# Opening of an attention and feed-forward kernel: k's first loads in requests of 16 tiles, row sums side by side in matmuls of 512, value products behind the gate's

## The chip, the cores and the metric

One core of one Trainium2 chip. The metric is device time in microseconds of one execution, about 810 us here. A profile is one further execution with its trace; its span (first to last instruction) is about 2 us shorter than the device time. "Seen at" is when an engine starts on loaded data, "landed" is when the load's completion packets are done in the trace, some 0.3 to 0.4 us earlier. "TensorE", "VectorE", "ScalarE" and "GpSimd" are PE, DVE, ACT and POOL in the profile's lines.

## The reference

Inputs are float32: q, k, v of 4 x 6016 x 256 and three feed-forward weights. Cut to what matters:

```python
qn = q / (np.linalg.norm(q, axis=1, keepdims=True) + 1e-06)   # norms over the 6016 rows
kn = k / (np.linalg.norm(k, axis=1, keepdims=True) + 1e-06)
s = kn.transpose(0, 2, 1) @ qn / tau                          # 256 x 256 per batch
a = softmax(s)                                                # written out in the original
x = (v @ a).reshape(B * S, D)
g = x @ w_gate
out = (silu(g) * (x @ w_val)) @ w_out
```

## The kernel before: the parts concerned

The softmax matrix is folded into the two feed-forward weights (Wg and Wv), so most of the time goes to three streams of matmuls: g_ps, v_ps and o_new. They can start only when batch 0's k and q have been loaded, their squares summed, k-transposed-q built, the softmax taken and the first weights folded. That is the opening, some 38 us, and only it is changed. Batches 1 to 3 do the same work in the background.

In the opening q and k are loaded as fp8, 47 tiles of 128 rows each. PSUM, below, is the memory in which the matmuls' results stand. VectorE and ScalarE square pairs of tiles in turn. A matmul with a matrix of ones sums the squares over the partitions:

```python
def first_row_sums(b, t, which, sq, t_last):
    if t == 0:
        ss_new = psum_gv.tile([P, C], FP32, tag="gv"[which])
        state[b, "ss", which] = ss_new
    pm = pairs[t][1]
    for s in range(pm):
        nc.tensor.matmul(state[b, "ss", which], ones_bf, sq[:, s, :],
                         start=(t == 0 and s == 0), stop=(t == t_last and s == pm - 1))

def first_row_copy(b):                       # q's sums so far, as one row
    row = work.tile([1, C], FP32, tag="row")
    nc.vector.tensor_copy(row, state[b, "ss", 0][0:1, :])
    state[b, "row"] = row
```

From q's sixth group on, the sums go into columns instead (`cols`): first the row is turned into columns by 1x1 matmuls, then each further square is added by one-column matmuls. So the row must be there before the last q groups can be summed. The order of loads and work:

```python
kgroups = [(s, min(8, NS - s)) for s in range(0, NS, 8)]   # 8,8,8,8,8,7 tiles
# qgroups come out as 8,8,8,8,4,4,4,2,1 tiles
order = [(g, 1, kgroups) for g in range(NG)] + [(g, 0, qgroups) for g in range(NQ)]
# ... all loads issued by GpSimd in this order, then v's first piece and the weights
G_COLS = NQ - 4
# per group of q: squares, gemm1_pair (k-transposed-q), sums; a reciprocal of k's norms after four of them
```

At the end of the softmax, the row sums of the exponentials and the first folded weights (units 0 and 1 are gate, 2 and 3 value):

```python
row_sum(0)
wp_matmul(b, 0, 0, units[0], lo)
wp_matmul(b, 1, 0, units[1], lo)
wp_matmul(b, 2, 0, units[2], lo)
row_sum(1)
finish_rs(b, rs)
for u, jh in ((0, 1), (1, 1), (2, 1), (3, 0), (3, 1)):
    wp_matmul(b, u, jh, units[u], lo)
```

## Time and profile before

| | before |
|---|---|
| device time, first three runs | 809.96 us median (809.69 to 813.19) |
| span in the profile | 807.6 us |
| TensorE busy | 787.9 us, 98% |
| chain that ended last | TensorE 95%, DMA 3% |
| first g_ps in the records | 37.64 us |
| first v_ps in the records | 37.85 us |

### The profile page before, as it was taken

What the parts mean: (1) busy time and instruction counts of PE and PEld (TensorE: products, weight loads), DVE (VectorE), ACT (ScalarE), POOL (GpSimd) and SP (SyncE); (2) the same over time, 40 slices, a digit from 0 to 9 for tenths busy, and PEclk for the clock granted to TensorE, in tenths of its full rate; (3) what the DMA queues carried; (4) which work ended last, traced back from release to release, by engine and by line L of the source; (5) the groups of instructions that cost most, each with busy time, mean ns of one, the idle gap of its engine ahead of it and who ended that gap; (6) DMA issues with size and microseconds to landing.
All of it is one profiled execution on the core that took longest, in us unless ns stands there. A gap on an engine that the chain in (4) does not pass through costs nothing.

```text
span 807.6 us, 11833 instructions
## 1 busy us (share of the span) xinstructions
PE 787.9 (98%) x3867; PEld 384.4 (48%) x3940; DVE 554.7 (69%) x854; ACT 454.3 (56%) x802; POOL 251.0 (31%) x302
## 2 busy tenths in 40 slices
PE   4999999999999999999999999999999999999998
PEld 3644444444454444444454444444445444444446
DVE  4777878758667878766766778766866665665654
ACT  4666666555556666555555656555555555555553
POOL 4415887332104786332000777610000000000000
PEclk8999999999999999999999999999999999999999
DMA  9995999799886685887976697667556665565443
GB/s 89 143 154 97 147 190 174 144 142 178 149 145 144 131 153 121 152 137 166 145 170 144 113 160 149 131 126 166 128 116 123 144 134 131 125 149 130 117 113 99
DMA packets 203567, 112.43 MB, mean 139 GB/s; under 512 B 151424, under 2 KB 190337, under 8 KB 202753
## 3 DMA queue, kind: packets, MB, share of 16 engines
q1 hardware_dynamic: 185456, 84.55, 44.1%
q0 software_dynamic: 17904, 27.01, 30.6%
q8 instruction: 31, 0.51, 0.3%
q14 instruction: 32, 0.25, 0.1%
q10 hardware_dynamic: 144, 0.10, 0.0%
HBM read 79.06 MB, written 60.48 MB: 173 GB/s over the span
## 4 chain that ended last, share of the span: by engine, by line
PE 95%; DMA 3%; issue 1%; ACT 0%; DVE 0%; POOL 0%; ACTq 0%; POOLq 0%
PE g_ps L458 30%; PE v_ps L458 30%; PE o_new L499 29%; PE ps L425 2%; DMA q_sb<-in_q_dram 2%; PE kq_new L171 2%; PE o_new L552 1%; DMA k_sb<-in_k_dram 1%; ACT silu L464 0%; DVE sv L468 0%; PE ss_new L198 0%; PE last_ps L576 0%; PE unit_ps L425 0%; PE kq_new L176 0%; PE ps L415 0%
## 5 line engine op out<-in xcount | busy, mean ns | idle before, releaser
L468 DVE TENSOR_TENSOR sv<-silu,v_ps 128x512 bf16<-128x512 bf16 (+1 forms) x576 | 386.5, 673 | 214.5 <-ACT silu L464 213.1
L464 ACT ACTIVATE silu<-g_ps 128x512 bf16<-128x512 f32 (+1 forms) x576 | 339.1, 589 | 292.5 <-PE g_ps L458 263.7
L458 PE MATMUL g_ps<-vT,Wg 128*128 128x512 bf16 (+1 forms) x1109 | 326.5, 375 | 1.2
L458 PE MATMUL v_ps<-vT,Wv 128*128 128x512 bf16 (+1 forms) x1104 | 325.1, 374 | 1.0
L499 PE MATMUL o_new<-sv,w_out_sb 128*128 128x512 bf16 (+1 forms) x1079 | 319.1, 375 | 1.4
L458 PEld LDWEIGHTS <-Wv 128*128 128x128 bf16 x1152 | 112.7, 98 | 130.9 <-ACT Wv L437 0.4
L303 POOL TENSOR_TENSOR acc_new<-acc_new,sq 128x512 f32<-128x512 f32 x135 | 157.2, 1165 | 52.6 <-DVE sq L293 37.3
L458 PEld LDWEIGHTS <-Wg 128*128 128x128 bf16 x1152 | 111.3, 98 | 125.8 <-DVE Wv L435 0.2
L499 PEld LDWEIGHTS <-w_out_sb 128*128 128x128 bf16 x1104 | 108.0, 98 | 126.5
L129 POOL DMA_DIRECT2D vb_new<-in_v_dram x47 | 24.2, 516 | 244.9 <-DMA vT<-vb_new 243.8
L509 DVE COPY pl<-o_new 128x512 uint16<-128x512 uint16 (+1 forms) x92 | 62.5, 680 | 14.1 <-ACT pl L508 13.9
L293 DVE TENSOR_TENSOR sq<-q_sb 128x512 bf16<-128x512 fp8e5 x72 | 65.8, 914 | 0.0
L508 ACT COPY pl<-o_new 128x512 uint16<-128x512 uint16 (+1 forms) x92 | 53.1, 578 | 19.8 <-PE o_new L499 19.1
L294 ACT ACTIVATE sq<-k_sb 128x512 bf16<-128x512 fp8e5 x72 | 44.2, 614 | 0.0
L171 PE MATMUL kq_new<-k_sb,q_sb 128*128 128x512 fp8e5 x184 | 28.4, 295 | 1.4 <-DMA q_sb<-in_q_dram 1.3
L114 POOL DMA_DIRECT2D q_sb<-in_q_dram x45 | 25.4, 564 | 11.7 <-DMA k_sb<-in_k_dram 9.8
L198 PE MATMUL ss_new<-sq,ones_bf 128*128 128x256 bf16 x83 | 14.8, 336 | 10.9 <-ACT sq L188 10.9
L171 PEld LDWEIGHTS <-q_sb 128*128 128x256 fp8e5 x184 | 21.2, 137 | 6.3 <-DMA q_sb<-in_q_dram 2.7
L114 POOL DMA_DIRECT2D k_sb<-in_k_dram x42 | 23.2, 554 | 2.9 <-DVE sv L468 1.7
L370 POOL TENSOR_SCALAR den<-th 128x512 f32<-128x512 f32 x3 | 1.8, 614 | 64.4 <-ACT th L369 64.4
L338 POOL TENSOR_TENSOR inv<-inv,half 64x8 f32<-64x8 f32 x3 | 5.0, 1665 | 53.3 <-DVE inv L336 53.3
L298 POOL TENSOR_TENSOR acc_new<-sq 128x512 f32<-128x512 bf16 x3 | 3.5, 1151 | 47.1 <-DVE sq L293 47.1
(90 smaller groups left out, 208.4 us busy)
## 6 DMA issues: line engine op xcount, KB each, us to landing
rows<-pl SPq DMA_DIRECT2D x86, 256.0 KB, 2.6
out_dram<-ot_new SPq DMA_DIRECT2D x43, 512.0 KB, 4.1
vb_new<-in_v_dram POOLq DMA_DIRECT2D x43, 256.0 KB, 4.8
q_sb<-in_q_dram POOLq DMA_DIRECT2D x36, 128.0 KB, 5.9
k_sb<-in_k_dram POOLq DMA_DIRECT2D x33, 128.0 KB, 7.4
ot_new<-rows SPq DMA_TRANSPOSE x92, 3.7
k_sb<-in_k_dram POOLq DMA_DIRECT2D x5, 256.0 KB, 9.0
rows<-pl SPq DMA_DIRECT2D x6, 192.0 KB, 2.4
```

Source lines behind the costliest of these rows:

```text
L114: nc.gpsimd.dma_start(out=dst[:, gs:gs + gm, :], in_=src[b].rearrange("(p s) c -> p s c", s=NS)[:, gs:gs + gm, :])
L129: nc.gpsimd.dma_start(out=vb[:mv, :].rearrange("(p s) c -> p (s c)", s=cm), in_=v[b, cs * P:cs * P + mv, :].rearrange("(p s) c -> p (s c)" ...
L171: nc.tensor.matmul(kq[:, jh, :], q_sb[:, ps:ps + 2, js], k_sb[:, ps:ps + 2, :], start=(t == 0 and jh == 0), stop=last, perf_mode=DR, skip_ ...
L293: nc.vector.tensor_mul(sq[:, :pm, 0, :], q_sb[:, ps:ps + pm, :], q_sb[:, ps:ps + pm, :])
L294: nc.scalar.activation(sq[:, :pm, 1, :], k_sb[:, ps:ps + pm, :], ACT.Square)
L303: nc.gpsimd.tensor_tensor(out=acc, in0=acc, in1=sq[:, s, :, :], op=ALU.add)
L458: nc.tensor.matmul(dst[:, :mv], W[:, kk, fs], vT[:, kk, :mv], start=(kk == 0), stop=(kk == CH - 1))
L464: nc.scalar.activation(silu[:, :mv], g_ps[:, :mv], ACT.Silu)
L468: nc.vector.tensor_mul(sv[:, f, :mv], silu[:, :mv], v_ps[:, :mv])
L499: nc.tensor.matmul(self.o_ps[h][:, :self.mv], w_out_sb[:, f, h * P:(h + 1) * P], self.sv[:, f, :self.mv], start=(f == 0), stop=(f == FH - 1))
L508: nc.scalar.copy(pl[:, 0, :self.mv], halves[:, 0, :self.mv])
L509: nc.vector.tensor_copy(pl[:, 1, :self.mv], halves[:, 1, :self.mv])
```

## The change

Its intent: fewer and larger load requests for k, half as many summing matmuls (each 512 wide, even and odd tiles side by side in one PSUM tile, added at the end), and the gate's folded weights finished before the value's. The large k groups are worked through in fours, so that the four square buffers suffice.

```diff
-            ss_new = psum_gv.tile([P, C], FP32, tag="gv"[which])
+            ss_new = psum_gv.tile([P, 2, C], FP32, tag="gv"[which])
...
-        for s in range(pm):
-            nc.tensor.matmul(state[b, "ss", which], ones_bf, sq[:, s, :],
-                             start=(t == 0 and s == 0), stop=(t == t_last and s == pm - 1))
+        nc.tensor.matmul(state[b, "ss", which][:, :pm, :], ones_bf, sq[:, :pm, :],
+                         start=(t == 0), stop=(t == t_last), skip_group_check=True)
...
-        nc.vector.tensor_copy(row, state[b, "ss", 0][0:1, :])
+        ss = state[b, "ss", 0]
+        nc.vector.tensor_copy(row, ss[0:1, 0, :])
+        nc.vector.tensor_add(row, row, ss[0:1, 1, :])
...
-        first_root(ink, state[b, "ss", 1])
+        ss = state[b, "ss", 1]
+        nc.vector.tensor_copy(ink, ss[:, 0, :])
+        nc.vector.tensor_add(ink, ink, ss[:, 1, :])
+        first_root(ink, ink)
...
-        wp_matmul(b, 2, 0, units[2], lo)
         row_sum(1)
         finish_rs(b, rs)
-        for u, jh in ((0, 1), (1, 1), (2, 1), (3, 0), (3, 1)):
+        for u, jh in ((0, 1), (1, 1), (2, 0), (2, 1), (3, 0), (3, 1)):
...
-    kgroups = [(s, min(8, NS - s)) for s in range(0, NS, 8)]
+    kgroups = [(s, min(16, NS - s)) for s in range(0, NS, 16)]
...
-        if n == 4:
+        if n == 3:
             make_identity(nc, identf)
...   (the loop over groups now takes the pairs of a group in fours: squares, products, sums)
```

More of the change, by code (lines that the diff above doesn't have):

```diff
@@ L680 @@
             first_row_copy(0)
-        sqs = [first_square(0, t, which, on_dve=(t % 2 == 1)) for t in ts]
-        if which == 0:
-            for t in ts:
-                gemm1_pair(0, t)
-            if g == G_COLS:
-                first_cols(0)
-            if g == NQ - 4:
-                keep_warm(1)
-        for t, sq in zip(ts, sqs):
-            if which == 0 and g >= G_COLS:
-                first_col_sums(0, t, sq)
-            else:
-                first_row_sums(0, t, which, sq, (T_COLS if which == 0 else NP) - 1)
+        for at in range(0, len(ts), 4):
+            now = ts[at:at + 4]
+            sqs = [first_square(0, t, which, on_dve=(t % 2 == 1)) for t in now]
+            if which == 0:
+                for t in now:
+                    gemm1_pair(0, t)
+                if g == G_COLS:
+                    first_cols(0)
+                    keep_warm(1)
+            for t, sq in zip(now, sqs):
+                if which == 0 and g >= G_COLS:
+                    first_col_sums(0, t, sq)
+                else:
+                    first_row_sums(0, t, which, sq, (T_COLS if which == 0 else NP) - 1)
         if which == 0:
```

## The prediction

> **What bounds the kernel now.** I read the page first (busy shares, chain by line), then the chain of waits in order of time for the first 70 us, then the timelines of VectorE and GpSimd for the first 40 us.
>
> From the page:
> ```profile
> span 807.6 us, 11833 instructions
> PE 787.9 (98%) x3867; PEld 384.4 (48%) x3940; DVE 554.7 (69%) x854; ACT 454.3 (56%) x802; POOL 251.0 (31%) x302
> PE 95%; DMA 3%; issue 1%; ACT 0%; DVE 0%; POOL 0%; ACTq 0%; POOLq 0%
> ```
> TensorE is the chain for 95% of the span. The change touches none of the matmuls of the three long lines (g_ps, v_ps, o_new); it touches only the opening, in which batch 0's k and q are loaded, squared and multiplied. So the question is by how much the start of the steady stream, the first g_ps, moves.
>
> From the chain of waits in order of time (start us, us, what), the opening:
> ```profile
> 1.93 7.03 DMA k_sb<-in_k_dram
> 9.24 19.08 DMA q_sb<-in_q_dram
> 28.36 1.09 PE kq_new L171 x8
> 29.44 0.89 PE ss_new L198 x8
> 30.33 0.44 PE kq_new L171 x4
> 30.77 0.47 PE ss_new L198 x4
> 31.26 0.42 DVE row L203
> 31.73 0.60 PE cols L211 x4
> 33.06 0.44 PE kq_new L171 x4
> 33.50 0.32 PE cols L221 x8
> ...
> 34.32 0.13 PE cols L221 x6
> ...
> 36.55 0.57 PE unit_ps L425 x5
> 37.12 0.47 PE ps L425 x4
> 37.64 0.38 PE g_ps L458
> ```
> Three stretches. To 28.3 us the loads set the pace. From 28.36 TensorE runs with no gap but one: at 31.26 it waits for VectorE's 0.42 us row copy. From 31.7 to the first g_ps at 37.64 it is continuous. A delay of the row copy therefore reaches the end of the kernel, unless the last q loads are later still.
>
> From VectorE's timeline, the stretch ahead of that copy:
> ```profile
> 22.86 0.29 DVE L233 TENSOR_SCALAR ink<-ink 128x256 f32<-128x256 f32 x1 [0.61 <-ACT ink L228]
> 23.58 1.29 DVE L185 TENSOR_TENSOR sq<-q_sb 128x512 bf16<-128x512 fp8e5 x2 [0.29 <-DMA q_sb<-in_q_dram]
> 28.43 1.29 DVE L185 TENSOR_TENSOR sq<-q_sb 128x512 bf16<-128x512 fp8e5 x2 [0.66 <-DMA q_sb<-in_q_dram]
> 30.65 0.54 DVE L238 RECIPROCAL ink<-ink 128x64 f32<-128x64 f32 x1
> 31.26 0.41 DVE L203 COPY row<-ss_new 1x256 f32<-1x256 f32 x1
> ```
> VectorE spends 1.29 + 0.55 = 1.84 us of each 2.46 us group of q and idles some 0.6; but from 28.43 to the copy it has almost no idle time, and its last reciprocal ends at 31.19, just ahead of the copy.
>
> **What the Trainium skill says.** (1) "DMA: Bandwidth & Descriptors", section "Where 436 GB/s comes from", puts the ceiling of the path into SBUF at 435.2 GB/s. TensorE sees q groups at 23.50, 25.94 and 28.36, so 2.43 us per 8 tiles, or 1.049 MB of float32 read: 432 GB/s. The trace agrees, so bigger requests can't make the stream much faster. (2) The same page's "Anatomy of one DMA" gives about 2 us fixed cost per DMA, mostly the receipt. Here that is hidden by requests queued behind: the last three 8-tile k groups are seen every 2.4 to 2.5 us, with no 2 us holes. (3) "TensorE: Matmul & The Clock Gate", section "Back-to-back issue gap", gives N/2.4 + 2.5 ns: 109 ns for 256 columns, 216 for 512. The chain has 0.89/8 = 111 ns, and 0.43/2 = 215 ns in the steady pairs. It agrees, so one matmul of 512 costs what two of 256 cost. (4) The same page's Part 1 has a clock that halves after sparse activity. The trace has a mean clock of 0.50 from 15 to 20 us, 0.87 from 20 to 25 and 1.00 after, so low only while loads pace the work.
>
> **The change part by part.**
>
> *k in 16s.* 3 loads in place of 6. The bytes are the same. A 7-tile group cost about 0.30 us less than an 8-tile one (its requests' landings 2.16 against 2.46 us apart), so 8 tiles are about 2.40 and a request costs some 0.05 us of its own, which is my estimate. Three fewer: q about 0.15 us earlier, the last k too. Against it: the first squares start one group later (about 9 in place of 6.56 us), and the last k group, now 15 tiles seen at about 18.4, needs 4 squares on each engine: 4 x 0.64 = 2.6 us on VectorE, to 21.0 at best, and 21.3 if its four square buffers wait for a slow TensorE. q's first group is seen at 20.85. So VectorE starts on q's squares at most 0.4 us late.
>
> *Sums side by side.* In the steady q groups 8 matmuls of 256 (0.89 us) become 4 of 512 (4 x 0.216 = 0.86): 0.03 saved. On the chain are one group of 8 and one of 4: about 0.05 us. The weight loads halve, but they are under the matmuls already.
> Two sums are added on VectorE. For k: a copy and an add of 128x256 float32, each about 0.42 (the 128x256 products from PSUM take 0.40 to 0.43). For q: an add of 1x256 behind the copy; a one-partition copy took 0.41, so I take 0.41.
> The k sums' chain: q's first squares end at 22.2 to 22.6, copy and add to 23.0 to 23.4, ScalarE's two passes 0.36 + 0.42 with hand-overs to 23.9 to 24.3, the addition of 1e-6 and the identity's cast to 24.5 to 24.9, where it was 23.29. From there VectorE is behind by about 1 us (second group at 24.5 to 24.9 in place of 23.58) and regains about 0.6 us a group: third group 26.35 to 26.75 in place of 26.02, fourth 28.2 to 28.6 in place of 28.43. It has caught up, or is 0.2 us late, just where the chain begins.
> From the fourth group: squares and reciprocal 1.80, one square 0.6, reciprocal 0.54, so 31.2 to 31.5, copy to 31.6 to 31.9, add to 32.0 to 32.3. The row was there at 31.67. So the row is 0.35 to 0.65 us late, and with it the 1x1 matmuls, the next square on VectorE and the rest of TensorE's continuous stretch.
>
> *Value product behind the gate's.* One matmul of 256 (0.11 us) moves from before to behind the second row sums. Before, it started at 36.25, when the second exponential was just done, so the sums came at 36.36; now they come about 0.07 us earlier. But TensorE is continuous there and has the same work before the first g_ps: 3+5+4 products become 2+6+4. Gate weights were ready at 37.34 and TensorE only free at 37.59, so the earlier scale is slack. I count 0.
>
> *Keep-warm and identity.* The first keep_warm stands in the same place in the stream. The identity is built after 4 issues, not 5; GpSimd had 8 requests out and then waited 1.9 us per issue, so it costs nothing.
>
> Sum at the row: +0.41 (second sum), 0.0 to +0.2 (VectorE's backlog), less what the earlier loads and the 0.05 of matmuls give: between +0.3 and +0.65. I take +0.4 us, unhidden in the TensorE-bound rest. 809.96 + 0.4 = 810.3, rounded down.
>
> **The rivals.**
> *A: the loads decide, gain.* If the last q landing, not the row, sets the end of the opening, the result is 0.15 to 0.3 us faster: about 809.7. For it: the last squares (33.76) did wait 0.30 us for q, so loads and TensorE are nearly level. Against it: TensorE had no gap there, and the row delay is larger than the gap.
> *B: a cold clock.* Bursts of 8 matmuls of 512 once per 4.9 us could leave the clock low at about 21 to 25 us. A cold q group needs some 1.75 + 1.7 us where 2.46 are given, a backlog of 1 us, which two warm groups of 1.95 us recover. If low past 28 us: +1 to +3 us, 811 to 813. Against it: TensorE is over 80% busy in q's groups, and before the clock rose under the same load.
> *C: a big request lands late.* If 16-tile requests are slower per byte or their last engine lags, q shifts by the excess; 5% of k's 14 us is 0.7 us, and 811. Nothing in the trace speaks for it: 1024-byte and 2048-byte packets took the same time per byte.
> *D: all is noise.* Three runs of before span 3.5 us, more than any effect here.
>
> **Range and chances.** The effect lies between -0.3 and +0.7 us in nearly all cases; runs add some 0.5, with an occasional run 3 us long that a median of few runs can catch, so the range is longer upwards: 809.0 to 812.2. Two per cent is 16 us; nothing in a 38 us opening of which 28 are loading gives that. Within 2%: 0.98; faster 0.01; slower 0.01.
>
> **What the changed profile would show.** Right: q's fourth group seen at about 28.2; the row's copy and its add back to back, ending 32.0 to 32.3; the chain passing through both; TensorE idle before the 1x1 matmuls; first g_ps about 0.4 us later, 38.0; the same spacing after it. Rival A: g_ps at or before 37.6, with the chain through q's last loads. Rival B: the clock below 1.00 between 25 and 30 us. C: the fourth group after 28.4. The prediction is wrong if VectorE idles before the row copy, or if the new add costs nearly nothing.

## More of the kernel before

One group of instructions in the opening, from the page's table of costly groups (line, engine, operation, output from inputs, shapes, count; busy us and mean ns of one; idle time before them and what ended it):

```profile
L198 PE MATMUL ss_new<-sq,ones_bf 128*128 128x256 bf16 x83 | 14.8, 336 | 10.9 <-ACT sq L188 10.9
```

These 83 recorded matmuls of 256 columns are the square sums of k and q. The idle time before them is TensorE waiting for squares, in effect for loads.

As markers of the end of the opening I use the first g_ps and the first v_ps in the records. Now and then a matmul record is missing, and the first v_ps proved the steadier of the two.

## The result

The changed kernel: 809.90 us median of 6 runs (809.37 to 813.62); before, 809.83 us median of 6 (809.33 to 813.19). The ratio is 1.0002, with a 95% interval of 0.9978 to 1.0026: the same. A ratio here is the mean time of one kernel's fast runs over that of the other's of the same rounds, so it is not quite the ratio of the medians. 810.3 was predicted.

The range that was predicted, 809.0 to 812.2, also holds the time of an unchanged kernel, so the number alone does not test the mechanism. The trace of the opening says what happened in one run of each kernel. The sums after, from the page's table of groups:

```profile
L197 PE MATMUL ss_new<-sq,ones_bf 128*128 128x512 bf16 (+1 forms) x42 | 13.6, 453 | 13.3 <-ACT sq L188 13.3
```

Half as many instructions, nearly the same busy time (13.6 in place of 14.8 us), more idle time before them. VectorE's timeline in the changed kernel, which answers to the one shown of before:

```profile
22.19 0.42 DVE L234 COPY ink<-ss_new 128x256 f32<-128x256 f32 x1
22.64 0.42 DVE L235 TENSOR_TENSOR ink<-ink,ss_new 128x256 f32<-128x256 f32 x1
...
24.33 1.29 DVE L185 TENSOR_TENSOR sq<-q_sb 128x512 bf16<-128x512 fp8e5 x2
...
28.23 1.29 DVE L185 TENSOR_TENSOR sq<-q_sb 128x512 bf16<-128x512 fp8e5 x2 [0.54 <-DMA q_sb<-in_q_dram]
...
31.07 0.41 DVE L203 COPY row<-ss_new 1x256 f32<-1x256 f32 x1
31.52 0.41 DVE L204 TENSOR_TENSOR row<-row,ss_new 1x256 f32<-1x256 f32 x1
```

VectorE falls behind at k's two new instructions, has caught up by 28.23 (it waits for q again), starts the row copy 0.19 us earlier than before and ends the new add at 31.93, 0.26 us later than the old copy. TensorE's timeline around it and at the end of the opening:

```profile
31.98 0.60 PE L212 MATMUL cols<-ones_f,row 1*128 1x1 f32 x4 [0.51 <-DVE row L204]
...
37.79 0.38 PE L461 MATMUL g_ps<-vT_new,Wg 128*128 128x512 bf16 x1
38.01 0.59 PE L461 MATMUL v_ps<-vT_new,Wv 128*128 128x512 bf16 x2
```

TensorE waits 0.51 us for the row's second sum, and the steady streams begin 0.15 to 0.16 us later than in the profile of before (37.64 and 37.85). So far the prediction's steps hold with a smaller sum, and the spans are equal (807.6 us both).

One sign that the prediction named is missing. The page's chain of the changed kernel does not pass through the row's copy and add, but through q's load, until 31.90, and a square on ScalarE:

```profile
31.98 0.64 ACT sq L188
32.62 0.12 issue
32.74 0.34 PE cols L222 x8
```

Such links are inferred, and this one misleads. The column sums at 32.74 are those of q's sixth group, and ScalarE squares its half of that group from 30.79 to 31.42. In "q's sums narrow" below, the same sums start at 32.33, while the square named here runs from 32.02 to 32.65. What the sums at 32.74 do follow is the 1x1 matmuls, by 0.75 to 0.76 us in each of the profiles of before, the changed kernel and the slow row, and these follow the row.

Why the loss is smaller than forecast, and why the times of either kernel fall into groups, the experiments have to tell.

### The profile page after: what moved, and what is told of

Its sections match the earlier page's. It is cut to its first block, busy times and chain, and to the rows that moved or that the text cites. A ratio compares the mean times of both kernels' runs of the same rounds, so it can differ in the third digit from the quotient of the medians.

```text
span 807.6 us, 11728 instructions
## 1 busy us (share of the span) xinstructions
PE 786.2 (97%) x3826; PEld 380.0 (47%) x3899; DVE 555.1 (69%) x857; ACT 454.6 (56%) x802; POOL 249.4 (31%) x299
## 3 DMA queue, kind: packets, MB, share of 16 engines
q0 software_dynamic: 17472, 27.01, 30.5%
## 4 chain that ended last, share of the span: by engine, by line
PE 94%; DMA 4%; issue 1%; ACT 1%; DVE 0%; POOL 0%; ACTq 0%; POOLq 0%
PE g_ps L461 30%; PE v_ps L461 30%; PE o_new L502 29%; PE ps L428 2%; DMA q_sb<-in_q_dram 2%; PE kq_new L171 2%; DMA k_sb<-in_k_dram 1%; PE o_new L555 1%; ACT silu L467 0%; DVE sv L471 0%; PE last_ps L579 0%; PE kq_new L176 0%; PE ps L418 0%; POOL k_sb L114 0%; PE cols L222 0%
## 5 line engine op out<-in xcount | busy, mean ns | idle before, releaser
L306 POOL TENSOR_TENSOR acc_new<-acc_new,sq 128x512 f32<-128x512 f32 x135 | 157.3, 1165 | 52.2 <-DVE sq L296 36.9
L197 PE MATMUL ss_new<-sq,ones_bf 128*128 128x512 bf16 (+1 forms) x42 | 13.6, 453 | 13.3 <-ACT sq L188 13.3
L114 POOL DMA_DIRECT2D k_sb<-in_k_dram x39 | 21.4, 550 | 1.1 <-POOLq L772 0.8
```

What stands on the lines that cost most here:

```text
L114: nc.gpsimd.dma_start(out=dst[:, gs:gs + gm, :], in_=src[b].rearrange("(p s) c -> p s c", s=NS)[:, gs:gs + gm, :])
L306: nc.gpsimd.tensor_tensor(out=acc, in0=acc, in1=sq[:, s, :, :], op=ALU.add)
```

## The experiments

All runs gave a correct result, all verdicts were "same" at 2%, and no run was of the slow state. Each kernel had five rounds (two have six times). The kernels of the table's last four rows ran on another chip (3) than those of the other experiments (8), each with runs of before beside it; for the two first profiles no chip is on record. This table has one profile per row. "Packet" is when the first 16,384-byte packet of the queue of kind "instruction" within the span starts; "last q" when the last data packet of q's first load has landed; "row" when VectorE's row is ready. The last column is the median of the kernel's runs.

| kernel | packet | last q | row | first v_ps | span | median |
|---|---|---|---|---|---|---|
| before, first profile | 30.59 | 33.31 | 31.67 | 37.85 | 807.6 | 809.83 |
| before again | 30.22 | 33.57 | 31.66 | 38.80 | 808.5 | 810.31 |
| changed, first profile | 35.85 | 32.64 | 31.93 | 38.01 | 807.6 | 809.90 |
| changed again | 35.69 | 32.65 | 31.96 | 38.74 | 808.3 | 809.94 |
| k in 16s alone | 30.10 | 33.45 | 31.47 | 38.67 | 809.5 | 809.74 |
| sums alone | 35.96 | 32.89 | 32.21 | 38.19 | 808.1 | 809.93 |
| value order alone | 30.27 | 33.65 | 31.67 | 38.98 | 809.9 | 810.57 |
| changed, q's sums narrow | 33.24 | 32.62 | 31.51 | 38.27 | 808.2 | 809.87 |
| changed, slow row | 37.35 | 32.55 | 33.12 | 39.64 | 809.3 | 811.90 |
| changed, columns earlier | 35.24 | 32.60 | 31.05 | 38.40 | 808.0 | 809.76 |
| changed, 82 more | 29.05 | 33.51 | 33.33 | 39.51 | 809.1 | 810.47 |
| changed, 150 more | 19.61 | 33.24 | 32.62 | 38.70 | 808.3 | 810.10 |
| changed, no warm-keeping | 35.75 | 32.70 | 32.03 | 37.71 | 807.7 | 809.61 |
| all together | 35.30 | 32.68 | 30.98 | 38.40 | 808.0 | 810.00 |

Span less first v_ps is 769.6 to 770.0 us in every row but two ("k in 16s alone" and "value order alone", 770.8 and 770.9, where TensorE later waits once for VectorE, 0.9 and 1.2 us). So the opening accounts for nearly all the difference between profiles, and the rest of the kernel is the same.

### The parts one by one

**k's loads in 16s alone** (the kernel before with the diff's last two hunks and the loop in fours).

> The kernel before with only k's loads in 16s (and the loop in fours that they need). Theory (two nearly level chains set the first gate product: VectorE's row of column sums with TensorE's work behind it, and q's last load): q's fourth group is seen at 28.2 in place of 28.36, the row copy ends at about 31.5 in place of 31.67, the first gate product starts at 37.4 to 37.55 in place of 37.64; total 0.1 to 0.25 us down, inside the noise. If TensorE's instruction stream is as long as before, the one 16 KB instruction packet again falls at about 30.5 us among q's last loads, and q's last data land at about 33.2; if it does not, at 32.6. Rival 'the loads don't matter': 37.64 unchanged.

Measured: 809.74 us median against 809.97, ratio 0.9995 (0.9982 to 1.0008). The row came at 31.47 and the fourth q group landed at 27.84 in place of 28.03, as expected: three requests fewer are worth about 0.19 us in this pair of profiles. But the first g_ps is at 38.46, far from the 37.4 to 37.55 expected. TensorE waited 1.14 us for q's sixth group, a wait that the first profile of before does not have.

**The sums alone** (the kernel before with the diff's first four hunks).

> The kernel before with only the sums side by side (both copies and adds on VectorE), loads in 8s. Theory: the second row sum adds 0.41 us behind the row copy, so the row is there at 32.0 to 32.2 in place of 31.67 and the first gate product starts at 37.8 to 38.1; total 0.2 to 0.45 us up. Rival 'the loads set the end alone': 37.64, or earlier. Because the instruction stream of TensorE is 82 rows shorter, the instruction packet should come after 33 us as in the changed kernel, and q's last data land by 32.8.

Measured: 809.93 against 809.97, ratio 1.0007 (0.9992 to 1.0023). Row at 32.21 (expected 32.0 to 32.2), first g_ps at 37.98 (37.8 to 38.1), packet at 35.96, last q at 32.89: all as expected or next to it. Against the first profile of before it costs 0.54 us at the row and 0.34 us at the first v_ps.

**The value product alone.**

> The kernel before with only the value product behind the gate's. Theory: TensorE is continuous there with the same work, so the row sums of the softmax come 0.05 to 0.1 us earlier but the first gate product starts at 37.6 to 37.7 as before; total unchanged. Rival: the earlier scale is on the path, then 37.5 or earlier.

Measured: 810.57 against 809.97, ratio 1.0007 (0.9995 to 1.0019); first g_ps at 38.76. This missed too: TensorE waited 1.10 us for q, ahead of the change's place. From the start of the last column sums to the first v_ps, however, the profiles can be compared, for no load interrupts that stretch in eight of them. With the old order it takes 3.69 (before), 3.61 (before again), 3.61 (k in 16s alone) and 3.61 (sums alone). With the new it takes 3.77 (value order alone), 3.72 (changed), 3.81 (82 more) and 3.71 (150 more). So the new order costs about 0.1 us, the length of the one matmul of 256 columns that used to run while TensorE waited for the second exponential.

### Repeats, and a wait that comes and goes

> The kernel before again, for the spread: first gate product at 37.64 give or take 0.1, the 16 KB instruction packet again at about 30.6 us and q's last data at 33.3 us if it belongs to TensorE's instruction stream; time 809.3 to 810.2 apart from an odd run 3 us longer. If the first gate product moves by more than 0.15 us between profiles of one kernel, the differences between kernels of that size are not to be read.

> The changed kernel again, for the spread: first gate product at 37.79 give or take 0.1, instruction packet at about 35.8 us, q's last data at 32.6; time 809.4 to 810.5 apart from an odd run 3 us longer.

Measured: before 810.31 us median of 6, the changed kernel 809.94 of 5, against 810.40 of the 11 runs of before in that call (ratios 1.0003 and 0.9994). The first v_ps moved by 0.95 us between two profiles of before, and by 0.73 us between two of the changed kernel, so neither was within 0.1. By the rule written there, then, differences of that size in the first g_ps say nothing between single profiles; only stretches without a load's wait can be compared so finely. TensorE's timeline of before, again:

```profile
32.29 0.65 PE L171 MATMUL kq_new<-k_sb,q_sb 128*128 128x512 fp8e5 x4 [1.08 <-DMA q_sb<-in_q_dram]
32.87 0.60 PE L211 MATMUL cols<-ones_f,row 1*128 1x1 f32 x4
```

The row was ready at 31.66, as in the first profile; yet the 1x1 matmuls start 1.14 us later than there, because the product ahead of them in TensorE's order waits 1.08 us for q's sixth group. In the first profile that group came in time. In the changed kernel, again, a different load is late:

```profile
37.86 0.61 PE L428 MATMUL ps<-w_gate_sb,exT 128*128 128x256 bf16 x4 [0.52 <-DMA w_gate_sb<-in_moe_w_gate_dram]
```

Beside each of these waits the trace has one packet of 16,384 bytes of the queue of kind "instruction". The DMA view of 30 to 31.6 us of before (first profile), and of 35.4 to 36.9 us of the changed kernel (queue, kind: packets, MB, share of the 16 engines):

```profile
q0 software_dynamic: 191, 0.16, 107.2%
q8 instruction: 1, 0.02, 3.7%
```

```profile
q0 software_dynamic: 388, 0.42, 165.3%
q8 instruction: 1, 0.02, 4.0%
```

Shares over 100% arise because packets in flight overlap in the record. In the openings of the fourteen profiles the instruction packet lasts 0.89 to 0.98 us (0.945 and 0.948 here), in the first of these windows 0.95/(16 x 1.6) = 3.7% of the 16 engines. The whole execution has 31 of them before and 30 after. The Trainium skill, "Runtime: NRT & Kernel Launch", section "Instruction fetch mechanics", says that an engine's instructions are fetched in blocks of 16 KiB, 256 instructions, and calls the cost "mostly hidden". The pages list 7807 matmuls and weight loads before and 7725 after (some records are missing), 30.5 and 30.2 blocks, so the counts agree with these packets being TensorE's. The spacing agrees too: from one packet to the next TensorE starts 217 to 295 of the recorded instructions in before, 251 on average, and VectorE and ScalarE fewer than 70 each.

That gave a new theory. The packet takes one engine out of a stream of loads that keeps all 16 busy, and the part of a load that is on that engine is late. The packet records fit this. q's last load is 128 packets of 256 bytes, eight for each of 16 engines if they share evenly. In the first profile of before 120 of them have ended by 32.78 us, and the last eight end one after the other from 33.02 to 33.31. In the changed kernel, where the instruction packet comes only at 35.85, all have ended by 32.64 with no such gap. In before the packet falls among q's last loads. In the changed kernel, with 82 TensorE instructions fewer, it falls among the weights.

The weight pieces order themselves by the packet as well. By their semaphores, the third piece lands at 37.48 to 37.81 in the three profiles whose packet starts at 35.24 to 35.69. In the three whose packet starts at 35.75 to 35.96 it lands at 36.26 to 36.47, and it is the piece behind it that is late, 1.65 to 1.75 us after it. With the packet at 30.59 or before, or at 37.35, the pieces land 0.6 to 0.8 us apart throughout.

Times agree that before has two groups. Of its 41 timed runs that are under 811 us, 16 lie from 809.16 to 809.97 and 25 from 810.20 to 810.96, none between. Its first profiled run (809.42) was of the lower group, the second (810.34) of the upper. The changed kernel's 11 are five of 809.37 to 809.64, four of 809.94 to 810.16, one of 810.49 and one of 813.62; its profiled runs were 809.37 and 810.09. What the runs at 813 are, no profile shows.

### Moving the packet on purpose

```diff
+    pad_ps = psum_o.tile([P, 2, C], FP32, tag="o")
+    for _ in range(41):          # 75 in the second kernel
+        nc.tensor.matmul(pad_ps[:, 0, 0:1], warm_bf[:, 0:P], ones_bf[:, 0:1], start=True, stop=True)
     G_COLS = NQ - 4
```

These run at the start, while TensorE waits for k anyway.

> The changed kernel with 41 idle one-column matmuls (82 instructions with their weight loads) in front of the first sums, while TensorE waits for k, so that its instruction stream is as long as before. Theory (new: one 16 KB instruction packet of TensorE's stream takes a DMA engine for 0.95 us and delays the load that is on that engine): the packet comes back to 30 to 31 us, q's fifth, sixth or last group lands 0.5 to 0.9 us late, TensorE waits for q where it did not, and the first gate product starts at 38.3 to 38.7 (37.8 if the packet just misses the fifth group). Rival 'loads in 16s and sums did away with the late q': packet elsewhere or harmless, q's last data at 32.6, first gate product at 37.8. Time within 0.8 us of the changed kernel's.

Measured: packet at 29.05, last q at 33.51, first g_ps at 39.08, 810.47 us median. In this run the loads landed 0.47 us later from the first on (k's first group at 9.09 in place of 8.62), which no theory had foreseen. The packet records show that it was not the whole stream: of the 128 packets of k's third load only one is late, at 18.52, where the others have ended by 18.02, and one of the first load's packets took 1.99 us, where the longest took 1.53 in the changed kernel. This points to one engine that was late from the start, with no instruction packet there; why is open. The shift is why the first g_ps lies beyond the expected 38.3 to 38.7. Beyond this common shift, q's fifth group is late by another 0.34 us (landed 29.94 against 29.13), and TensorE waits for it:

```profile
31.12 0.65 PE L171 MATMUL kq_new<-k_sb,q_sb 128*128 128x512 fp8e5 x4 [0.48 <-DMA q_sb<-in_q_dram]
```

> The same with 75 such matmuls (150 instructions). Theory: the packet comes at 24 to 27 us, among q's groups of 8. If an engine never catches up, every later landing is about 0.6 us late, q's last data at 33.2, first gate product at 38.3 to 38.6 in every run. If the engines share what is lost and catch up, q's last data are at 32.6 to 32.9 and the first gate product at 37.8 to 38.0.

Measured: packet at 19.61, earlier than the 24 to 27 expected, 810.10 us median. The k groups landed as in the changed kernel (8.51, 13.37, 17.94); from then on every one of q's first four landings is 0.60 to 0.61 us later than there (21.11, 23.57, 26.03, 28.48 against 20.51, 22.97, 25.42, 27.88). The last q data came at 33.24, also 0.60 later. So the lost time is not made up for 13 us. All five times lie close together (809.86 to 810.27). First g_ps 38.27 against 38.3 to 38.6 expected, and first v_ps 0.69 us later than in the changed kernel's first profile. The two padded kernels support the theory. The instruction stream's length moves the packet, and later loads are then about 0.6 us late. In the second kernel, of the 128 packets of q's last load, 120 have ended by 32.53, as in the changed kernel, and the last eight end from 32.95 to 33.24. So one sixteenth of the load is late, the share of one engine. That it is the engine that fetched is inferred; the records do not name engines.

### Is the row on the path?

**Four more copies of the row.**

```diff
         nc.vector.tensor_add(row, row, ss[0:1, 1, :])
+        for _ in range(4):
+            nc.vector.tensor_copy(row, row)
```

> The changed kernel with four more copies of the row onto itself on VectorE behind the add, the answer the same. Theory (the row is on the path): each copy of 1x256 float32 costs 0.2 to 0.4 us, the first gate product moves by the whole sum less at most 0.15, so from 37.79 to 38.5 to 39.3, and the total rises by the same 0.8 to 1.5 us, which five rounds should show. Rival 'the loads set the end': less than 0.3 us.

Measured: 811.90 us median, ratio to before 1.0020 (1.0008 to 1.0032), the one kernel clear of noise. VectorE's and TensorE's timelines:

```profile
31.89 1.23 DVE L206 COPY row<-row 1x256 f32<-1x256 f32 x4
```

```profile
33.17 0.60 PE L214 MATMUL cols<-ones_f,row 1*128 1x1 f32 x4 [1.77 <-DVE row L206]
```

The row is 1.19 us later than in the changed kernel, the 1x1 matmuls 1.19 us later, the first v_ps 1.63 us later, and the time is 1.96 us above the changed kernel's median in the same call. The loads do not hide the row: the last column sums start 1.19 us later too (35.48 against 34.29), so a delay of the changed kernel's row is on the path in full. The size is above the expected 0.8 to 1.5. Some 0.35 of the excess is a new wait of TensorE for the exponentials, behind a small VectorE scalar add of 128x2 that took 0.60 us there and 0.17 elsewhere; why is open.

**q's sums narrow again, no second sum.**

```diff
+        if which == 0:
+            for s in range(pm):
+                nc.tensor.matmul(state[b, "ss", which][:, 0, :], ones_bf, sq[:, s, :],
+                                 start=(t == 0 and s == 0), stop=(t == t_last and s == pm - 1))
+            return
...
-        nc.vector.tensor_add(row, row, ss[0:1, 1, :])
```

> The changed kernel with q's sums narrow again (matmuls of 256) and without the second row sum; k's sums stay wide, loads in 16s. Theory: the row is there at 31.4 to 31.6 in place of 31.93, the end of the opening is then q's last load (32.64), and the first gate product starts at 37.35 to 37.5 in place of 37.79; total 0.3 us down against the changed kernel, below what rounds can show. Rival 'the row's add is hidden': 37.79 unchanged.

Measured: 809.87 us, ratio to before 0.9997 (0.9985 to 1.0009). The row came at 31.51 and the last q at 32.62, both as expected, and the 1x1 matmuls start at 31.57, 0.41 us earlier than in the changed kernel: the add's whole length. The last column sums start 0.41 us earlier as well (33.88). Yet the first v_ps is at 38.27, later. The narrow sums are 36 instructions more, the packet came at 33.24, and v's first piece, next in the queue, was late:

```profile
35.54 0.62 PE L150 MATMUL vt_ps<-ident,v_sb 128*128 128x128 bf16 x8 [0.82 <-DMA v_sb<-in_v_dram]
```

What the row gained was lost in a new wait.

### What lies behind

**Columns from one load earlier** (G_COLS is NQ - 5 in place of NQ - 4).

> The changed kernel with the row taken one load earlier: from the fifth q group on the sums go straight to columns. Theory: the row is ready near 30.9 us, while two loads are still to come, so the add is hidden and only q's last load (about 32.6) and then the weights' landings set the end: first gate product at 37.0 to 37.4 in place of 37.79, total 0.4 to 0.8 us down. Rival 'the row was not on the path': 37.7 to 37.8 unchanged. If the weights' landings take over (the fourth weight piece lands at about 36.6), nearer 37.4.

Measured: 809.76 us, ratio 0.9994 (0.9982 to 1.0006); row at 31.05, first g_ps at 37.97, first v_ps at 38.40. The first g_ps was expected at 37.0 to 37.4, so this is a miss: the packet at 35.24 met the weights, and TensorE waited 0.29 us for the third piece.

**Without the five keep-warm matmuls.**

> The changed kernel without its five keep-warm matmuls (10 instructions fewer). Theory: the packet moves from 35.7 to 36.0 or later, behind the third weight piece's landing at 35.9, so the wait for weights seen in one of two profiles (0.52 us) is gone; the row at 31.9 still sets the end, and the first gate product starts at 37.6 to 37.85; times gather near 809.5 in place of two groups near 809.5 and 810.1. Rival 'the clock needs them': a clock of 0.5 shortly after 35 us and 1 to 3 us lost.

Measured: 809.61 us median, all five runs at 809.53 to 810.07, ratio 0.9993 (0.9979 to 1.0006), the lowest median of all kernels; before had 810.31. The first v_ps is the earliest of all, 37.71, and no clock record falls below full speed between 24 us and the last 3 us. The packet came at 35.75, not at 36.0 or later, and the wait for weights was not gone: it moved to the next piece, as the chain of waits shows.

```profile
32.94 7.34 DMA w_gate_sb<-in_moe_w_gate_dram
40.28 0.04 issue
40.32 0.59 PE ps L426 x2
```

**That kernel, with one reduction for the row and columns earlier.**

> That kernel with the row summed by one reduction over both halves in place of a copy and an add, and the row taken one load earlier. Theory: the row is off the path, q's last data (32.6) set the end, the packet comes near 35.9; first gate product at 37.2 to 37.5, total 0.3 to 0.6 us under the changed kernel's best runs, if the packet misses the third weight piece; with it, 37.9 to 38.1.

Measured: 810.00 us, ratio 0.9996 (0.9983 to 1.0008). The row was ready at 30.98, almost 1 us earlier than in the changed kernel, the packet came at 35.30, and TensorE waited 0.60 us for the third weight piece:

```profile
37.53 0.60 PE L426 MATMUL ps<-w_gate_sb,exT 128*128 128x256 bf16 x4 [0.60 <-DMA w_gate_sb<-in_moe_w_gate_dram]
```

With the row out of the way the first v_ps is at 38.40, in the branch that the expectation gave for a packet that meets the weights. (The first g_ps record there is at 37.97; where the records hold both of the first pair, as here, it stands 0.43 us ahead of the first v_ps, and 0.21 where they hold one, as in before. So it reads up to 0.22 us early beside 37.64.) No kernel is faster than both by more than the noise; the one without keep-warm matmuls comes nearest.

## Why the prediction was right

It said 810.3 within 809.0 to 812.2; 809.90 was measured. The total is right mainly because the opening is small and the range wide: the 0.4 us that the prediction forecast lies within the runs' scatter, and the medians differ by 0.07. So the number does not confirm the mechanism; the traces confirm part of it. That the waits which the change removes and brings leave the time where it was, was not foreseen: that part is luck. By its own steps:

- **Loads a little earlier: right.** Three requests fewer were taken as 0.15 us. q's fourth group was seen at 28.18 (28.2 was written) and landed 0.15 us earlier in the changed kernel, 0.19 with the loads changed alone.
- **VectorE falls behind and catches up: right.** The second q group's squares started at 24.33 where 24.5 to 24.9 were written, the fourth at 28.23.
- **The second row sum on the path: right in kind, a little too large.** The row was to be 0.35 to 0.65 us late, at 32.0 to 32.3; it came at 31.93, 0.26 late, because VectorE had caught up fully and the earlier loads counted: the row copy itself started 0.19 us earlier than before. The add cost 0.41 us, as written, and in the changed kernel a row 0.41 us earlier (q's sums narrow) or 1.19 later (slow row) moves the last column sums by just as much. Of its signs, the end of the add (32.0 to 32.3) and the first g_ps (38.0) came 0.07 and 0.21 us early, and the page's chain did not pass through the row, by a link that the timelines contradict. VectorE did not idle before the row copy (its reciprocal runs from 30.45 to 30.99), which would have spoken against it.
- **Value product, "I count 0": wrong, +0.1 us.** Total work until the first g_ps is the same, but in the old order one matmul ran inside a wait. The step failed by adding up work and overlooking that a gap had been in use.
- **"Unhidden in the TensorE-bound rest": too strong.** Rival A had seen that loads and TensorE were nearly level, and it was partly right. The first profile of before had its last q data at 33.31, and the change's at 32.64. From the 1x1 matmuls to the start of the last column sums the changed kernel needed 34.29 - 31.98 = 2.31 us where before needed 34.16 - 31.73 = 2.43. So 0.12 of the 0.25 us by which the 1x1 matmuls are late came back. With the 0.03 us between 3.69 and 3.72 in the stretch after, that makes the observed 0.16 at the first v_ps. (The value order's cost of 0.1 is the difference of the groups; this one profile of before is the slowest of its four there.)
- **"TensorE had no gap there": true of that profile, not of the kernel.** It was a run of the lower group. In the upper group, 25 of its 41 runs, TensorE should have the wait for q of 1.1 us; the profiles that show it are the repeat and the two single-part kernels with the same packet place. The change moves the packet by 5.3 us, out of q's loads, so it exchanges that wait for one of about 0.5 us for weights, seen in one of its two profiles. The prediction had neither, and where before has its wait the exchange works against the loss it forecast. Whether the change gains some tenths of a microsecond on average is not settled: the ratio was 1.0002 and 0.9994, both intervals holding 1.
- **Rivals B and C: fell.** The clock was full from 23.0 us on in the first profile of the changed kernel, and the 16-tile requests landed without an excess.
- **A reading of the stream's rate: wrong.** The 432 GB/s are the float32 bytes read. What enters SBUF is fp8, a quarter of that: the profile of before has 104 to 107 GB/s from 10 to 30 us. So they can't be held against a limit of the path into SBUF; which limit holds is not shown. That larger requests gain little is measured: 0.15 to 0.19 us for three fewer.

## What to carry to other kernels

In a stretch where several chains are nearly level, here VectorE's row, q's last loads, v and the weight pieces, shortening one only uncovers the next, and a single profile shows just one of the orders in which they can end. Look at the times' groups, and profile twice, before reading a gap of under 1 us. With the DMA engines full, as here, the program's own length mattered: when a block of instructions was fetched decided which load was late, so adding or removing instructions far from the path can move a wait onto it. And work moved out of a wait in which it used to run is no longer free: here 0.1 us for one matmul.

## What the Trainium skill lacked or had wrong

- "Runtime: NRT & Kernel Launch", section "Instruction fetch mechanics", calls the cost of a fetch "mostly hidden" and does not speak of other loads. Here the 16,384-byte packet of the opening took 0.89 to 0.98 us, later landings were 0.60 us late for 13 us (150 more instructions), and TensorE waited 0.3 to 1.1 us for q, v or weights. (That the packet is the cause of each of these waits is inferred from its place.)
- "DMA: Bandwidth & Descriptors", section "Anatomy of one DMA", gives about 2 us fixed cost per DMA and there no figure for requests queued one behind another. Here three requests fewer moved the fourth q group's landing by 0.15 to 0.19 us, so each cost 0.05 to 0.06 us of its own.
- No page looked up here says that executions of one kernel on one core can fall into two groups, 809.2 to 810.0 and 810.2 to 811.0 us, by where such a packet meets the loads. The link of group and packet is inferred: most of these runs have a time but no trace.
